# Moving the turn of the next queries and the expert-count step within a fused attention and expert-gate kernel

## The chip, the cores and the metric

The kernel runs on one core of a Trainium2 chip. The metric is the device time of one execution in microseconds (us). A profiled execution records every instruction of TensorE (matrix products), VectorE, ScalarE, GpSimd (called POOL in the profile) and SyncE (SP), and the transfers of the DMA engines. Each engine works through its own list of instructions in the order in which the program issues them, and waits at an instruction until what it needs is there.

## The reference, in short

Attention with 16 query heads over one key head and one value head, for 8 batches of 384 tokens and head dimension 64, and after it a layer of experts with two gates:

```
scores = q @ k.T / 8            # per batch b and head h: 384 x 384
attn   = softmax(scores)
x      = (attn @ v), heads side by side           # 3072 tokens x 1024
group  = argmax(x @ w_group)                      # 4 groups
expert = argmax(x @ w_expert[group])              # 4 experts in each
weight = softmax weight of group * softmax weight of expert
out    = weight * (relu(x @ w1[expert]) @ w2[expert])
```

Each token goes to one of 16 experts, each with two 1024 x 1024 matrices.

## The kernel before, in words

The attention is cut into 48 groups of 1024 score columns, two groups `g = 2p` and `g + 1` to a pair `p`, and three pairs to a batch: pair `p` is number `r = p % 3` of batch `b = p // 3`. The loop over `p` (L385) goes to 24; pass 24 only finishes pair 23. The schedule is written out by hand: instructions run on each engine in the order of the source.

What one pair does, with the helpers' names and lines:

- `load_q` (L78) brings the raw queries in on SP's queue, three pairs ahead (four transfers, three buffers); it is issued at the end of a pass, behind `stats_q` (L155, ScalarE, a sum of squares that also reads the queries). `prep_q` (L176) is VectorE's block transpose ("the turn") of the raw queries into `qT` (two buffers), which the scores of that pair need. `prep_k` (L169) does the same for the keys of a batch, `kT`, once in three pairs. `load_kv` (L85, L88) issues keys and values on ScalarE's queue at the end of each first pair of a batch.
- `scores(g, kt)` (L185, L187): score matmuls into a PSUM tile (two buffers), then ScalarE's exponential into a tile `pt` (eight buffers). There are three such calls for a group.
- `pre_add(g, 1)` (L195) and `pre_add(g, 2)` (L199): VectorE adds up the three `pt` tiles of a group into `presum`. `fold_keys(g)` (L207, L211): a block transpose `turn` and a reduction `fold`.
- `values(g)` (L232): the value matmuls of a group into `o`, two PSUM banks with one buffer. The gate's small matmuls (`gps`, `cps`, outside the unit stage `lps`) use the same buffer.
- `invert(p)` (L216 to L220): four small matmuls `sm` that need both `fold` halves of the pair, a reciprocal `rc` and its spreading `rinv`, both on VectorE. `weigh(p)` (L240, L241): VectorE multiplies `o` by `rinv` into `xT`, which frees `o`; GpSimd casts it to `xbf`.

The gate of batch `b - 1` runs in three steps during batch `b`: `gate_a` (L252, L254) in the pass with `r = 0`; `gate_b` (L261 to L293: logits, one-hot and weights) right behind it in passes below 7, and in the pass with `r = 1` otherwise; `gate_c` (L297 to L317) in the pass with `r = 1`. `gate_c` is the expert-count step: a matmul `cps` into the buffer of `o`, its reduction `cnt` on VectorE, the most frequent expert by a maximum and its index, a register load on GpSimd with the transfers of that expert's two matrices `w1` and `w2` (three transfers on GpSimd's queue, L93 and L307), and some further small VectorE instructions.

From pass 7 on (`busy`, `MOE_AT = 7`) units of the expert layer are put between: `fill(n)` issues the next `n` units, each eight matmuls (`hps` L329 or `yps` L338) and one ScalarE instruction. A batch has 14 units, and they begin with the first batch's.

The order within a pass, before the change: scores of `g`, two calls; L195; the values of the previous pair, with `sm`, `rc`, `rinv`, `xT` (in passes below 7 two score calls stand between the value groups); the third call of `g` and the first of `g + 1`; L199, `turn`, `fold` of `g`; `prep_q`; the last two score calls of `g + 1`; then the gate steps, `prep_k` and `fold_last` (L195, L199, `turn`, `fold` of `g + 1`), whose mutual order the diff shows.

Of the kernel before, what the change touches and what calls it, by code (L numbers as in the profile page):

```python
# [21 lines left out]
def kernel(  # L22
# [12 lines left out]
    B, H, S, D = q.shape  # L35
# [55 lines left out]
    def load_w1(w1, e):  # L91
        for a in range(2):
            nc.gpsimd.dma_start(out=w1[a * D:(a + 1) * D], in_=w1f[bass.ds(e, 1), a].rearrange("e p k f -> (e p) k f"))  # L93
# [73 lines left out]
    def prep_k(b):  # L167
        kT[b] = pool.tile([P, S], FP32, tag="kT", name="kT")
        nc.vector.transpose(out=kT[b][:], in_=k_raw[b][:].rearrange("p k d -> p (k d)"))  # L169

    def prep_q(p, parts=1):
        t = pool.tile([P, 2 * CW], FP32, tag="qT", bufs=2, name="qT")
        src = q_raw[p][:].rearrange("p k d -> p (k d)")
        w = 2 * CW // parts
        for i in range(parts):
            nc.vector.transpose(out=t[:, i * w:(i + 1) * w], in_=src[:, i * w:(i + 1) * w])  # L176
        qT[2 * p] = t[:, 0:CW]
        qT[2 * p + 1] = t[:, CW:2 * CW]

    def scores(g, kt):  # L180
        b = g // NCH
        ps = ps_s.tile([P, 2, CW], FP32, tag="s", name="s")
        for par in range(2):
            r = slice(64 * par, 64 * par + 64)
            nc.tensor.matmul(out=ps[:, par, :], lhsT=kT[b][r, kt * P:(kt + 1) * P], rhs=qT[g][r, :], start=True, stop=True)  # L185
        t = pool.tile([P, 2, CW], FP32, tag="pt", bufs=8, name="pt")
        nc.scalar.activation(out=t[:], in_=ps[:], func=ACTF.Exp, scale=scale)  # L187
        pt[g, kt] = t
# [3 lines left out]
    def pre_add(g, kt):  # L192
        if kt == 1:
            t = pool.tile([P, 2, CW], FP32, tag="presum", bufs=1, name="presum")
            nc.vector.tensor_add(out=t[:], in0=pt[g, 0][:], in1=pt[g, 1][:])  # L195
            presum[g] = t
        elif kt == 2:
            t = presum[g]
            nc.vector.tensor_add(out=t[:], in0=t[:], in1=pt[g, 2][:])  # L199
# [13 lines left out]
    def invert(p):  # L213
        sm = ps_m.tile([P, 32], FP32, tag="mm", name="sm")
        for par in range(2):
            nc.tensor.matmul(out=sm[64 * par:64 * par + 64, :], lhsT=sel2[:].rearrange("p a b -> p (a b)"), rhs=fold[p][:, :, 16 * par:16 * par + 16], start=True, stop=True)  # L216
        rc = pool.tile([P, 32], FP32, tag="rc", name="rc")
        nc.vector.reciprocal(out=rc[:], in_=sm[:])  # L218
        t = pool.tile([P, 2 * CW], FP32, tag="rinv", bufs=1, name="rinv")
        nc.vector.transpose(out=t[:].rearrange("p (b i) -> p b i", i=32), in_=rc[:].unsqueeze(2).to_broadcast([P, 32, 32]))  # L220
        rinv[p] = t
# [3 lines left out]
    def values(g):  # L225
        b = g // NCH
        p, ch = divmod(g, 2)
        if ch == 0:
            o_ps[p] = ps_o.tile([P, 2, CW], FP32, tag="o", name="o")
        for kt in range(ST):  # L230
            for par in range(2):
                nc.tensor.matmul(out=o_ps[p][64 * par:64 * par + 64, ch, :], lhsT=v_sb[b][:, kt, :], rhs=pt[g, kt][:, par, :], start=(kt == 0), stop=(kt == ST - 1))  # L232
# [62 lines left out]
    def gate_c(b):  # L295
        ps = ps_o.tile([P, ST, GE], FP32, tag="o", name="cps")
        nc.tensor.matmul(out=ps[:].rearrange("p s e -> p (s e)"), lhsT=ones_bf[:], rhs=ohe_t[b][:].rearrange("p s g e -> p (s g e)"), start=True, stop=True)  # L297
        cnt = pool.tile([P, GE], FP32, tag="cnt", bufs=1, name="cnt")
        nc.vector.reduce_sum(out=cnt[:], in_=ps[:].rearrange("p s e -> p e s"), axis=AX)  # L299
        top = pool.tile([P, 8], FP32, tag="top", bufs=1, name="top")  # L300
        idx = pool.tile([P, 8], U32, tag="idx", bufs=2, name="idx")
        nc.vector.max_with_indices(out_max=top[:], out_indices=idx[:], in_=cnt[:])
        reg = nc.values_load(idx[0:1, 0:1], engines=(ET.Pool,), min_val=0, max_val=GE - 1, skip_runtime_bounds_check_because="an index into 16 counts")
        w1 = wpool.tile([P, KO, F], BF16, tag="w1", name="w1")
        load_w1(w1, reg)
        w2 = wpool.tile([P, FO, Dm], BF16, tag="w2", name="w2")
        nc.gpsimd.dma_start(out=w2[:], in_=w2f[bass.ds(reg, 1)].rearrange("a p k f -> (a p) k f"))  # L307
        wts[b] = (w1, w2)
        idf = pool.tile([P, 1], FP32, tag="idf", bufs=1, name="idf")
        nc.vector.tensor_copy(out=idf[:], in_=idx[:, 0:1])  # L310
        mask = pool.tile([P, GE], FP32, tag="mask", bufs=1, name="mask")
        nc.vector.tensor_scalar(out=mask[:], in0=iota16[:], scalar1=idf[:, 0:1], scalar2=None, op0=OP.is_equal)
        nc.vector.scalar_tensor_tensor(out=extra[:, b * GE:(b + 1) * GE], in0=cnt[:], scalar=0.0, in1=mask[:], op0=OP.is_gt, op1=OP.subtract)
        gm = pool.tile([P, ST, GE], FP32, tag="gm", bufs=1, name="gm")
        nc.vector.tensor_mul(out=gm[:], in0=gate_all[:, b * GE:(b + 1) * GE, :].rearrange("p e s -> p s e"), in1=mask[:].unsqueeze(1).to_broadcast([P, ST, GE]))
        gs = pool.tile([P, ST], FP32, tag="gsel", bufs=4, name="gsel")
        nc.vector.reduce_sum(out=gs[:], in_=gm[:], axis=AX)  # L317
        gsel[b] = gs
# [40 lines left out]
    NP = NFLAT // 2  # L359
# [14 lines left out]
    def fill(n):  # L374
        while n > 0:
            if not units:
                if begun[0] >= B or begun[0] not in wts:
                    return
                units.extend(first_units(begun[0]))
                begun[0] += 1  # L380
            units.pop(0)()
            n -= 1

    MOE_AT = 7
    for p in range(NP + 1):  # L385
        b, r = divmod(p, RP)
        g = 2 * p
        busy = p >= MOE_AT
        if p < NP:
            scores(g, 0)  # L390
            scores(g, 1)
            pre_add(g, 1)
        else:
            fill(2)
        if p > 0:
            values(g - 2)
            if busy:
                values(g - 1)
                invert(p - 1)
        if p < NP:  # L400
            scores(g, 2)
            scores(g + 1, 0)
        if p > 0:
            if not busy:
                values(g - 1)
                invert(p - 1)
            weigh(p - 1)
        units_on = busy and p < NP

        if not busy:  # L410
            if p < NP:
                pre_add(g, 2)
                fold_keys(g)
            if p + 1 < NP:
                prep_q(p + 1)
        elif p < NP:
            if r == 1:
                gate_b(b - 1, between=True)
            fill(1)
            pre_add(g, 2)  # L420
            fold_keys(g)
            if p + 1 < NP:
                prep_q(p + 1)
            fill(1)
        if p < NP:
            scores(g + 1, 1)
            scores(g + 1, 2)


        def fold_last():  # L430
            if p < NP:
                pre_add(g + 1, 1)
                pre_add(g + 1, 2)
                fold_keys(g + 1)

        if not busy:
            if r == 2 and b + 1 < B:
                prep_k(b + 1)
                stats_k(b + 1)
            if r == 0 and 0 < b < B:  # L440
                gate_a(b - 1)
                gate_b(b - 1)
            if r == 1 and b > 0:
                gate_c(b - 1)
            fold_last()
        elif p < NP:
            if r == 2 and b + 1 < B:
                prep_k(b + 1)
            fold_last()
            fill(1)  # L450
            if r == 2 and b + 1 < B:
                stats_k(b + 1)
            fill(1)
            if r == 0 and 0 < b < B:
                gate_a(b - 1)
            if r == 1 and b > 0:
                gate_c(b - 1)
            fill(p % 2)
            assert not inserts
        if r == 0 and b + 1 < B:  # L460
            load_kv(b + 1)
        if p < NP:
            stats_q(p)
            if p + 3 < NP:
                load_q(p + 3)
# [254 lines left out]
```

## Time and profile before

| What | Value |
|---|---|
| Timed runs (2) | median 571.74 us, 570.04 to 573.44 |
| Profiled execution, whole time | 569.86 us |
| Its span | 567.9 us |
| TensorE matmuls busy | 496.1 us (87%) |
| VectorE busy | 369.9 us (65%) |
| ScalarE busy | 242.0 us (43%) |
| GpSimd busy | 63.8 us (11%) |
| Mean granted TensorE clock | 0.947 |

The span is the time from the first to the last recorded instruction; the whole time is a little longer. A busy share is an average over stages. Which engine sets the time of a stage is read from the waits and the timeline of that stage, not from the shares. The granted clock is given as a share of 2.4 GHz, so 0.50 is the level of 1.2 GHz.

### The profile page before, as it was taken

What the parts mean: (1) busy time and instruction counts of PE and PEld (TensorE: products, weight loads), DVE (VectorE), ACT (ScalarE), POOL (GpSimd) and SP (SyncE); (2) the same over time, 40 slices, a digit from 0 to 9 for tenths busy, and PEclk for the clock granted to TensorE, in tenths of its full rate; (3) what the DMA queues carried; (4) which work ended last, traced back from release to release, by engine and by line L of the source; (5) the groups of instructions that cost most, each with busy time, mean ns of one, the idle gap of its engine ahead of it and who ended that gap; (6) DMA issues with size and microseconds to landing.
All of it is one profiled execution on the core that took longest, in us unless ns stands there. A gap on an engine that the chain in (4) does not pass through costs nothing.

```text
span 567.9 us, 6824 instructions
## 1 busy us (share of the span) xinstructions
PE 496.1 (87%) x2521; PEld 210.1 (37%) x2521; DVE 369.9 (65%) x503; ACT 242.0 (43%) x342; POOL 63.8 (11%) x64
## 2 busy tenths in 40 slices
PE   6758677857979997999899998999899979989992
PEld 4222222313434342433443343434343434454550
DVE  2865776796979848775978496787788567241100
ACT  2434225233536444444634562556355435232331
POOL 0010011111011101110021002010111011010000
PEclk8798788879999998999999998999999989999997
DMA  9450223892359843986199529943697129689990
GB/s 122 44 67 0 38 70 47 136 213 74 59 72 216 213 96 43 199 176 160 39 165 201 171 47 143 208 154 85 99 210 176 46 45 206 176 189 236 237 253 16
DMA packets 148377, 73.06 MB, mean 129 GB/s; under 512 B 122587, under 2 KB 122587, under 8 KB 148336
## 3 DMA queue, kind: packets, MB, share of 16 engines
q0 software_dynamic: 19008, 37.84, 36.8%
q1 hardware_dynamic: 114928, 32.53, 27.1%
q10 hardware_dynamic: 14400, 2.16, 2.1%
q8 instruction: 23, 0.38, 0.3%
q14 instruction: 18, 0.15, 0.1%
HBM read 91.31 MB, written 19.40 MB: 195 GB/s over the span
## 4 chain that ended last, share of the span: by engine, by line
PE 67%; DVE 22%; issue 4%; DMA 2%; ACT 2%; SPq 1%; POOL 0%; DVEq 0%; POOLq 0%; ACTq 0%
PE o L232 23%; PE s L185 19%; PE yps L338 12%; PE hps L329 10%; DVE turn L207 4%; DVE presum L199 4%; DVE qT L176 3%; DVE presum L195 2%; DVE rinv L220 2%; DVE xT L240 2%; DMA out_dram<-y 2%; DVE fold L211 2%; PE gps L252 2%; ACT y L340 1%; DVE oh L278 1%
## 5 line engine op out<-in xcount | busy, mean ns | idle before, releaser
L187 ACT ACTIVATE pt<-s 128x1024 f32<-128x1024 f32 x144 | 140.1, 1020 | 175.0 <-PE s L185 174.9
L185 PE MATMUL s<-qT,kT 64*128 64x512 f32 x576 | 155.0, 659 | 35.6 <-DVE qT L176 17.6
L232 PE MATMUL o<-pt,v 128*64 128x512 f32 x576 | 139.8, 634 | 16.0 <-DVE cnt L299 16.0
L329 PE MATMUL hps<-xbf,w 128*128 128x384 bf16 x512 | 89.3, 326 | 2.2 <-ACT hT L331 0.9
L338 PE MATMUL yps<-w,hT 128*128 128x512 bf16 x384 | 89.5, 379 | 1.3 <-ACT y L340 1.3
L185 PEld LDWEIGHTS s<-qT,kT 64*128 64x128 f32 x576 | 53.7, 199 | 96.9 <-issue 79.6
L232 PEld LDWEIGHTS o<-pt,v 128*64 128x64 f32 x576 | 41.0, 145 | 115.3 <-issue 90.2
L195 DVE TENSOR_TENSOR presum<-pt 128x1024 f32<-128x1024 f32 x48 | 57.8, 1205 | 36.6 <-ACT pt L187 36.4
L241 POOL CAST xbf<-xT 128x1024 bf16<-128x1024 f32 x24 | 40.8, 1699 | 350.7 <-DVE xT L240 350.7
L329 PEld LDWEIGHTS <-w 128*128 128x128 bf16 x512 | 48.5, 99 | 48.1 <-issue 18.5
L207 DVE STREAM_TRANSPOSE turn<-presum 128x1024 f32<-128x1024 f32 x48 | 59.8, 1245 | 1.6
L199 DVE TENSOR_TENSOR presum<-presum,pt 128x1024 f32<-128x1024 f32 x48 | 58.6, 1221 | 2.9 <-DVE presum L195 0.5
L211 DVE TENSOR_REDUCE fold<-turn 128x32 f32<-128x1024 f32 x48 | 58.6, 1220 | 1.6
L218 DVE RECIPROCAL rc<-sm 128x32 f32<-128x32 f32 x24 | 8.6, 358 | 77.4 <-PE sm L216 77.4
L338 PEld LDWEIGHTS <-hT 128*128 128x128 bf16 x384 | 37.0, 100 | 51.9 <-issue 14.1
L340 ACT ACTIVATE y<-yps,gsel 128x512 f32<-128x512 f32 x48 | 32.9, 686 | 54.2 <-PE yps L338 49.3
L331 ACT ACTIVATE hT<-hps 128x384 bf16<-128x384 f32 x64 | 31.3, 490 | 40.2 <-PE hps L329 32.9
L176 DVE STREAM_TRANSPOSE qT<-qraw 128x1024 f32<-128x1024 f32 (+1 forms) x25 | 29.7, 1191 | 3.6 <-DMA qraw<-in_q_dram 3.6
L155 ACT ACTIVATE junk<-qraw 128x1024 bf16<-128x1024 f32 x24 | 25.2, 1052 | 14.5 <-DMA k<-in_k_dram 14.4
L220 DVE STREAM_TRANSPOSE rinv<-rc 128x1024 f32<-128x1024 f32 x24 | 29.9, 1245 | 0.8
L240 DVE TENSOR_TENSOR xT<-o,rinv 128x1024 f32<-128x1024 f32 x24 | 29.4, 1224 | 1.3
L93 POOL DMA_DIRECT2D w<-in_moe_w_dram x18 | 12.6, 706 | 101.3 <-DVE gsel L317 76.7
(123 smaller groups left out, 161.1 us busy)
## 6 DMA issues: line engine op xcount, KB each, us to landing
w<-in_moe_w_dram POOLq DMA_DIRECT2D x18, 1024.0 KB, 13.3
w<-in_moe_w_dram POOLq DMA_DIRECT2D x9, 2048.0 KB, 23.7
qraw<-in_q_dram SPq DMA_DIRECT2D x96, 128.0 KB, 3.8
out_dram<-y SPq DMA_DIRECT2D x48, 256.0 KB, 3.4
x_bf<-xbf SPq DMA_DIRECT2D x8, 768.0 KB, 3.4
k<-in_k_dram ACTq DMA_DIRECT2D x28, 48.0 KB, 2.2
v<-in_v_dram ACTq DMA_DIRECT2D x8, 96.0 KB, 2.6
xe<-x_bf SPq DMA_DIRECT2D x1, 768.0 KB, 9.5
```

Source lines behind the costliest of these rows:

```text
L176: nc.vector.transpose(out=t[:, i * w:(i + 1) * w], in_=src[:, i * w:(i + 1) * w])
L185: nc.tensor.matmul(out=ps[:, par, :], lhsT=kT[b][r, kt * P:(kt + 1) * P], rhs=qT[g][r, :], start=True, stop=True)
L187: nc.scalar.activation(out=t[:], in_=ps[:], func=ACTF.Exp, scale=scale)
L195: nc.vector.tensor_add(out=t[:], in0=pt[g, 0][:], in1=pt[g, 1][:])
L199: nc.vector.tensor_add(out=t[:], in0=t[:], in1=pt[g, 2][:])
L207: nc.vector.transpose(out=t[:], in_=presum[g][:].rearrange("p a n -> p (a n)"))
L211: nc.vector.reduce_sum(out=fold[p][:, ch, :], in_=t[:].rearrange("p (b i) -> p b i", i=32), axis=AX)
L220: nc.vector.transpose(out=t[:].rearrange("p (b i) -> p b i", i=32), in_=rc[:].unsqueeze(2).to_broadcast([P, 32, 32]))
L232: nc.tensor.matmul(out=o_ps[p][64 * par:64 * par + 64, ch, :], lhsT=v_sb[b][:, kt, :], rhs=pt[g, kt][:, par, :], start=(kt == 0), stop=(kt ...
L241: nc.gpsimd.tensor_copy(out=xbf[b][:, cs], in_=xT[b][:, cs])
L329: nc.tensor.matmul(out=ps[:, 0:S], lhsT=w1[:, ko, fc * P:(fc + 1) * P], rhs=xb[:, ko * S:(ko + 1) * S], start=(ko == 0), stop=(ko == KO - 1))
L338: nc.tensor.matmul(out=ps[:], lhsT=state["h"][:, fo, st * P:(st + 1) * P], rhs=w2[:, fo, nh * CW:(nh + 1) * CW], start=(fo == 0), stop=(fo ...
```

## The change

`prep_q(p + 1)` and, in the last pair of a batch, `prep_k(b + 1)` are issued right behind the first key addition of the pass (L195 of `g`), in all passes with a next pair. Before, `prep_q` stood behind `fold` of `g` and `prep_k` ahead of `fold_last`. `stats_k` stays where it was. In passes from 7 on with `r = 1`, `gate_c` is issued ahead of `fold_last` and ahead of the units that follow; before, it stood behind `fold_last` and two units. Nothing that is computed changes.

```diff
             scores(g, 0)
             scores(g, 1)
             pre_add(g, 1)
+            if p + 1 < NP:
+                prep_q(p + 1)
+            if r == 2 and b + 1 < B:
+                prep_k(b + 1)
         else:
             fill(2)
...
             if p < NP:
                 pre_add(g, 2)
                 fold_keys(g)
-            if p + 1 < NP:
-                prep_q(p + 1)
         elif p < NP:
             if r == 1:
                 gate_b(b - 1, between=True)
             fill(1)
             pre_add(g, 2)
             fold_keys(g)
-            if p + 1 < NP:
-                prep_q(p + 1)
             fill(1)
...
         if not busy:
             if r == 2 and b + 1 < B:
-                prep_k(b + 1)
                 stats_k(b + 1)
...
         elif p < NP:
-            if r == 2 and b + 1 < B:
-                prep_k(b + 1)
+            if r == 1 and b > 0:
+                gate_c(b - 1)
             fold_last()
             fill(1)
             if r == 2 and b + 1 < B:
                 stats_k(b + 1)
             fill(1)
             if r == 0 and 0 < b < B:
                 gate_a(b - 1)
-            if r == 1 and b > 0:
-                gate_c(b - 1)
             fill(p % 2)
```

## Rows read from the trace of the kernel before

**Rows 1.** Waits of TensorE: us in total, times, longest us.

```profile
PE s L185 <- DVE qT L176: 17.6, 7, 6.0
PE o L232 <- DVE cnt L299: 16.0, 6, 3.0
PE s L185 <- DVE kT L169: 12.9, 2, 6.5
PE s L185 <- DVE cnt L299: 4.7, 1, 4.7
```

**Rows 2.** Timeline, one early pair: start us, us, engine, line; idle before in brackets.

```profile
107.96 1.99 PE L185 MATMUL s<-qT,kT 64*128 64x512 f32 x8
109.88 2.79 PE L232 MATMUL o<-pt,v 128*64 128x512 f32 x12
...
112.81 0.36 DVE L218 RECIPROCAL rc<-sm 128x32 f32<-128x32 f32 x1 [3.28 <-PE sm L216]
...
114.48 1.22 DVE L240 TENSOR_TENSOR xT<-o,rinv 128x1024 f32<-128x1024 f32 x1
...
119.29 1.23 DVE L176 STREAM_TRANSPOSE qT<-qraw 128x1024 f32<-128x1024 f32 x1
120.45 0.53 DVE L169 STREAM_TRANSPOSE kT<-k 128x384 f32<-128x384 f32 x1
...
121.13 3.79 PE L185 MATMUL s<-qT,kT 64*128 64x512 f32 x8 [6.45 <-DVE kT L169]
```

**Rows 3.** Windows: stretch, busy us by engine, granted clock, DMA share, GB/s.

```profile
119.00:123.00 4.00, 1.87 (x5) 0.94 (x7) 3.90 (x5) 0.00 (x0) 0.00 (x0) 0.50 1.17 214
...
127.00:131.00 4.00, 4.00 (x18) 1.17 (x16) 0.24 (x1) 1.94 (x2) 0.00 (x0) 1.00 0.71 106
```

**Rows 4.** Chain of waits, value matmuls in passes 8 and 11: start us, us.

```profile
163.86 5.37 PE o L232 x24
...
223.36 7.07 PE o L232 x24
```

**Rows 5.** Timeline of VectorE: count step and last key additions of pair 4.

```profile
101.71 0.17 DVE L299 TENSOR_REDUCE cnt<-cps 128x16 f32<-128x48 f32 x1
...
103.32 1.22 DVE L195 TENSOR_TENSOR presum<-pt 128x1024 f32<-128x1024 f32 x1
...
108.32 1.22 DVE L195 TENSOR_TENSOR presum<-pt 128x1024 f32<-128x1024 f32 x1
```

**Rows 6.** Timeline: first L195 of pair 1, and `sm` of pair 6.

```profile
25.45 1.23 DVE L195 TENSOR_TENSOR presum<-pt 128x1024 f32<-128x1024 f32 x1
...
147.49 0.26 PE L216 MATMUL sm<-fold,sel 128*64 128x32 f32 x4
```

**Rows 7.** Timeline of pair 6: gate computation's start, what follows it, next exponentials.

```profile
140.24 0.18 DVE L273 COPY L<-lps 128x60 f32<-128x60 f32 x1
...
142.24 1.22 DVE L195 TENSOR_TENSOR presum<-pt 128x1024 f32<-128x1024 f32 x1
...
144.68 1.92 ACT L187 ACTIVATE pt<-s 128x1024 f32<-128x1024 f32 x2
```

**Rows 8.** Timeline of TensorE, scores ahead of pass 11.

```profile
218.37 1.99 PE L185 MATMUL s<-qT,kT 64*128 64x512 f32 x8 [0.86 <-DVE qT L176]
```

**Rows 9.** Timeline of TensorE, first scores of passes 4 and 7.

```profile
81.50 3.78 PE L185 MATMUL s<-qT,kT 64*128 64x512 f32 x8 [1.83 <-DVE qT L176]
...
140.37 1.99 PE L185 MATMUL s<-qT,kT 64*128 64x512 f32 x8 [1.79 <-DVE qT L176]
```

**Rows 10.** DMA issues: line, count, KB each, median us to landing.

```profile
w<-in_moe_w_dram POOLq DMA_DIRECT2D x9, 2048.0 KB, 23.7
```

**Rows 11.** Timeline, query loads on SP's queue and pair 5's sum of squares ending.

```profile
99.69 28.72 SPq L78 DMA_DIRECT2D qraw<-in_q_dram  x5
...
117.31 0.19 ACT L155 ACTIVATION_READ_ACCUMULATOR junk<-qraw 128x1 f32 x1
```

**Rows 12.** The raw queries' tile: its transfers.

```profile
DMA to landing us min/median/max: 2.4/3.8/11.9
```

## The prediction

> **What bounds the kernel now.** I read the waits of TensorE first, because TensorE is the busiest engine of the page. Nearly all its long waits in the attention loop end on VectorE: 17.6 us on `qT` (L176), 12.9 on `kT` (L169), 16.0 and 4.7 on `cnt` (L299) [rows 1]. So the question is what stands in front of these three in VectorE's program order, and the timeline of VectorE answers it.
>
> The loop has two stages. In pairs 0 to 6 no expert units run. There the timeline of one pair [rows 2] reads as one chain: `rc` at 112.81, five more VectorE steps (`rinv`, `xT`, second key addition, `turn`, `fold`), `qT` at 119.29, `kT`, and only then TensorE's next scores at 121.13, after 6.45 us without a matmul. Those eight score matmuls take 3.79 us where eight earlier ones took 1.99: the granted clock is 0.50 (the 1.2 GHz level) in the stretch that follows the idle one, and 1.00 (2.4 GHz) four microseconds on [rows 2, 3]. The scores need nothing of `rc` to `fold`; they stand behind them only through `qT`.
>
> In pairs 7 to 23 expert units fill TensorE. The chain of waits [rows 4] passes there through the 24 value matmuls `o` of the pair after each count step. They wait for `cnt` because counts and values share one PSUM buffer, and `cnt` stands behind the five steps of the last key additions. Six such waits make the 16.0 us [rows 1]. Three of the six `o` groups then take 7.07 us instead of 5.37.
>
> **The change, part by part, pairs 0 to 6.** `prep_q` moves ahead of `rc`. Its load was issued two pairs earlier and its destination was last read by scores that precede those feeding L195, so I cost the turn at its own 1.23 us and no wait (bounded under the rivals). What is late next? With `qT` early, TensorE may run the next pair's first two scores right behind this pair's last two. VectorE then has no idle time left, because what it waited for, `sm`, comes while it is adding and turning. One round of VectorE, step by step:
> - L195 1.22 [rows 5] and `qT` 1.23 [rows 2];
> - `rc` to the end of `fold`: 119.29 - 112.81 = 6.48 [rows 2];
> - the second group's L195, L199, `turn`, `fold`: 108.32 - 103.32 = 5.00 [rows 5];
> - sum 13.93 us.
>
> TensorE needs less: three times 1.99 for scores and twice 2.79 for values, 11.6 us [rows 2]. Placing it against `rc` at T: its scores end by about T+2, values wait for `xT` at T+2.9 (114.48 + 1.22 - 112.81) [rows 2], and 2.79 + 1.99 + 2.79 later, at T+10.5, it waits for the last `fold` at T+11.5. Two gaps of about 1 us each, off VectorE's path. ScalarE's six exponentials and one sum of squares fit between.
>
> From the first L195 of pair 1, at 25.45, to `sm` of pair 6, at 147.49, the old kernel takes 122.0 us [rows 6]. The new one: 6 x 13.93 = 83.6; two `kT` at 0.53 make 1.1 [rows 2]; two gate computations of 142.24 - 140.24 = 2.0 make 4.0 [rows 7]; one count step 103.32 - 101.71 = 1.6 [rows 5]. In pair 3 the exponentials for pair 4 stay behind the gate's own: they end 6.4 us after `L` starts (144.68 + 1.92 - 140.24) [rows 7], the first near T+11.9; a score, six values and `sm` follow, T+16.8, where VectorE would be ready at T+15.9: 0.9 more. In pair 6 both value groups precede those scores, so nothing. Sum 91.2: a gain of **30.8 us**. Pair 0 does the same VectorE work in another order and gains nothing before 25.45.
>
> **Pairs 7 to 23.** `qT` in front of `rc` costs 1.23 us on VectorE, `kT` 0.53 in one pair of three. The cover is the 5.37 us of value matmuls during which `rc` waits for `sm` [rows 4]. Without it `xT` comes 1.8 us later, and next wanted is its PSUM buffer, by the count matmul or the next values, more than 10 us on. So nothing. `prep_k` moved needs keys loaded two pairs ahead: nothing.
>
> `gate_c` moves ahead of the last additions on VectorE, and on TensorE ahead of two or three units. The new wait is `cps` for the gate's one-hot; behind it on TensorE stand those units. The gate computation follows `xT` directly and TensorE has two units and two scores in between, so I cost it at nothing; unhidden it would be a few tenths, six times. Its Pool part moves along: one register load and three weight transfers, issued about 5 us earlier, behind which the next `xbf` cast stands with over 10 us to spare. SP's queue is passed by nothing. On VectorE the 1.6 us [rows 5] now delay `fold`, hence `sm`. But `cnt` comes 5 us earlier and the values behind it take 5.37 us, in which L195 to `fold` (5.00) fits, just.
>
> Gone are therefore the six waits, 16.0 us [rows 1]; the low clock behind three of them, 3 x (7.07 - 5.37) = 5.1 [rows 4]; and one wait of scores for `qT`, 0.9 [rows 8]. That makes **22.0 us**.
>
> **The sum.** 30.8 + 22.0 = 52.8. The profiled execution took 569.86 us (its span of 567.9 and 1.96 around it); 569.9 - 52.8 = 517.1. The median of the two timed runs stands 1.9 above that execution.
>
> **The clock, weighed.** The low level costs an early pair 1.8 us on eight scores [rows 2]; with the values after it at most about 3. It follows long idle stretches as a rule, but the rows hold two pairs with the gate's matmuls, where three shorter gaps, the last of 1.83 and 1.79 us, precede the scores: once these take 3.78 us, once 1.99 for eight [rows 9]. My early pairs leave two gaps of about 1 us, and one of about 3 ahead of the gate's matmuls in pairs 3 and 6. I take full clock except half a us each in those two pairs, rounding 517.1 up to 518, and keep 6 x 3 = 18 us as the other end. The Trainium skill, page "TensorE: Matmul & The Clock Gate", section "A second HAM failure mode: psum-queue depth-cycling", speaks against me: it reports that short idles between groups of matmuls, repeated often enough, also make the clock swing. By that rule the sum would come out near 530 instead of 517; the low start at 81.50 agrees with it, the full one at 140.37 does not, so the trace leaves it open.
>
> **Rivals.**
> 1. The clock drops in every early pair. TensorE's round becomes 11.6 + 3 = 14.6, above VectorE's 13.93, and the delays add to the handovers: 3 to 18 us more, 520 to 535. For it: most old early pairs start low. Against: those follow gaps of up to 6 us [rows 1], mine are of about 1.
> 2. The first expert's weights are late. Pair 7's first unit needs them. They are issued right after pair 4's `cnt`, which in my schedule is 25.45 + three rounds + 8.93 of the fourth (up to its `fold`) + 0.5 for `kT` + 2.9 for the gate of pair 3 = 79.6 us, and land 23.7 us later at the median [rows 10], near 105; the unit starts near 118. Only if the transfer took over 38 us would the early gain be given back. Price: up to some 10 us, 527.
> 3. The reciprocal's delay reaches TensorE after all: 23 turns at 1.23 and seven `kT` at 0.53, together 32 us, on the path: 549. For it: `xT` holds the buffer that values need. Against: after `sm` TensorE has four scores to run, about 4 us, more than `xT`'s 2.9 and nearly all of it.
> 4. Slower: the turn waits for its queries and VectorE, in order, holds `rc`, `xT` and both additions behind it. For it: query loads issued beside the weights drag on; the five from 99.69 take 28.72 us to issue, the longest landing is 11.9 [rows 11, 12]. From the end of the square sum that lets the last four go (117.31 + 0.19) to the latest landing, 99.69 + 28.72 + 11.9 = 140.3, are 22.8 us. In my schedule `rc` of pair 5 starts at 89.2 by the same sum and the squares end some 3.4 later, 92.6; the turn wants the queries at 25.45 + 91.2 + 1.2 = 117.8: 25 us, 2 us to spare. This decides from there: if each of the 23 turns waited 3 us, 69 us would come on top, 586. Against: most loads land in 3.8 us [rows 12], and the weights are under way in less than half of each three pairs.
> 5. Another engine's order keeps the old pace: the scores are really held by something else that ends when `qT` does. Then about 22 us or less remain, 548 to 565. Against: 121.13 follows `kT` immediately, and the waits name it.
>
> **Chances and range.** Forecast 0.70 (own range 511 to 524: half a us per early pair either way, the gate pairs, and the cover of `cnt`), rival 1 0.14, rival 2 0.03, rival 3 0.05, rival 4 0.03, rival 5 0.05. Two per cent, 11 us, is about what a measurement can tell from no change. Faster by more: the forecast, rivals 1 to 3 and over half of rival 5, 0.94; within: 0.03; slower: 0.03. For 8 in 10 I take the forecast's low end and rival 1 to its upper end: 509 to 534.
>
> **What would show it.** In the changed profile: `qT` right behind L195, and `rc` with almost no idle time before it in pairs 1 to 6; `sm` of pair 6 near 117; rounds of 14 us; a full clock there; no value matmul waiting for `cnt`; every `o` group of 24 at 5.37. I am wrong if the early rounds stay near 20 us, if `qT` waits for a transfer, or if the values now wait for `xT` in the unit pairs.

## The result and the profile after

The changed kernel takes 525.03 us (median of two runs, 524.29 and 525.78) against 571.74; the ratio is 0.918, interval 0.909 to 0.927. In a later group of four runs it took 523.42 us against 574.33: 0.910, interval 0.908 to 0.913. The forecast of 518 is 7 us too low, inside its range of 509 to 534. The profiled execution took 524.29 us, 7.2 more than the 517.1 of the sum.

The waits answer [rows 1] first (engine and line that waited, for whom: us in total, times, longest):

```profile
DVE qT L176 <- DMA qraw<-in_q_dram: 31.5, 6, 7.0
...
DVE rc L218 <- PE sm L216: 10.4, 4, 7.1
...
PE yps L338 <- DVE rc L218: 5.1, 4, 2.1
PE s L185 <- DVE qT L176: 3.6, 1, 3.6
...
PE o L232 <- DVE cnt L299: 1.7, 1, 1.7
...
PE hps L329 <- DVE L L273: 1.1, 2, 0.9
...
PE s L185 <- DVE kT L169: 0.6, 1, 0.6
```

Of the waits of [rows 1] little is left: 3.6 us on `qT`, which are the first load of all, 0.6 on `kT`, and 1.7 for `cnt`, in pair 4. Two things are new: VectorE waits 31.5 us for raw queries, where it waited 3.6 before, and TensorE's units wait 5.1 us for `rc`.

Now the early pairs, beside [rows 2, 5, 6], from the timeline (start us, us, engine, line; idle before in brackets):

```profile
25.24 1.22 DVE L195 TENSOR_TENSOR presum<-pt 128x1024 f32<-128x1024 f32 x1
...
86.30 1.22 DVE L195 TENSOR_TENSOR presum<-pt 128x1024 f32<-128x1024 f32 x1
...
87.43 1.24 DVE L176 STREAM_TRANSPOSE qT<-qraw 128x1024 f32<-128x1024 f32 x1
...
88.59 0.54 DVE L169 STREAM_TRANSPOSE kT<-k 128x384 f32<-128x384 f32 x1
89.05 0.32 DVE L218 RECIPROCAL rc<-sm 128x32 f32<-128x32 f32 x1
...
89.62 2.04 PE L185 MATMUL s<-qT,kT 64*128 64x512 f32 x8 [0.27 <-ACT pt L187]
...
100.48 1.22 DVE L195 TENSOR_TENSOR presum<-pt 128x1024 f32<-128x1024 f32 x1
...
117.16 0.31 PE L216 MATMUL sm<-fold,sel 128*64 128x32 f32 x4
```

A round of VectorE, from one first addition to the next, is 100.48 - 86.30 = 14.18 us, `kT` in it; no instruction of it waits. The next pair's scores start 0.57 us after `rc` does, after 0.27 us of idle time and at 2.04 us for eight. `sm` of pair 6 stands at 117.16, where 116.7 was worked out. The clock of the busy stretches is full (windows: stretch, busy us by engine, granted clock, DMA share, GB/s):

```profile
88.00:98.00 10.00, 9.44 (x44) 2.90 (x42) 9.76 (x10) 7.35 (x10) 1.97 (x1) 1.00 1.15 212
160.00:180.00 20.00, 20.00 (x109) 7.95 (x108) 14.35 (x13) 10.08 (x13) 1.97 (x1) 1.00 0.54 148
```

The new waits are in the unit stage. Passes 13 to 15 of the changed kernel, from the timeline:

```profile
243.37 1.37 POOL L93 DMA_DIRECT2D w<-in_moe_w_dram  x2 [6.84 <-DVE gsel L317]
...
244.87 20.51 SPq L78 DMA_DIRECT2D qraw<-in_q_dram  x4
...
266.88 0.26 PE L216 MATMUL sm<-fold,sel 128*64 128x32 f32 x4
...
271.44 1.25 DVE L176 STREAM_TRANSPOSE qT<-qraw 128x1024 f32<-128x1024 f32 x1 [6.95 <-DMA qraw<-in_q_dram]
272.61 0.32 DVE L218 RECIPROCAL rc<-sm 128x32 f32<-128x32 f32 x1
272.98 1.89 PE L338 MATMUL yps<-w,hT 128*128 128x512 bf16 x8 [2.09 <-DVE rc L218]
```

And the kernel before, at the same two steps of pass 13 (the loads, and the weights behind them):

```profile
281.50 2.27 SPq L78 DMA_DIRECT2D qraw<-in_q_dram  x4
...
285.57 1.37 POOL L93 DMA_DIRECT2D w<-in_moe_w_dram  x2 [12.96 <-DVE gsel L317]
```

Before, the four query transfers of this pass were issued within 2.27 us and the weights 4 us later. Now the weights come 1.5 us ahead, and the four take 20.51 us to issue. The longest landing of a query transfer rose from 11.9 [rows 12] to 25.1 us:

```profile
DMA to landing us min/median/max: 2.4/3.8/25.1
```

The Trainium skill, page "Trainium Kernel Development and Optimization", section "Key Constraints", says that transfers issued from SP, ScalarE and GpSimd run on the same 16 DMA engines and interleave; 20.51 us against 2.27 agrees. Two passes later the turn wants these queries and waits 6.95 us. `sm` has been ready since 267 and `rc`, behind the turn, comes at 272.61. `sm` lies in one of the two PSUM buffers that the units use as well, so the unit's matmuls wait for `rc`.

### The profile page after: what moved, and what is told of

The parts are those of the page before. It is cut to its first block, busy times and chain, and to the rows that moved or that the text cites. A ratio compares the mean times of both kernels' runs of the same rounds, so it can differ in the third digit from the quotient of the medians.

```text
span 522.3 us, 6814 instructions
## 1 busy us (share of the span) xinstructions
PE 480.7 (92%) x2521; PEld 203.6 (39%) x2521; DVE 369.3 (71%) x503; ACT 240.5 (46%) x342; POOL 63.8 (12%) x64
## 4 chain that ended last, share of the span: by engine, by line
PE 49%; DMA 18%; DVE 15%; SPq 7%; ACT 4%; issue 4%; ACTq 1%; POOL 0%; DVEq 0%; POOLq 0%
DMA qraw<-in_q_dram 15%; PE yps L338 13%; PE s L185 12%; PE hps L329 12%; PE o L232 9%; SPq L78 6%; PE gps L252 3%; DVE qT L176 2%; DVE presum L195 2%; DVE turn L207 2%; DMA out_dram<-y 2%; DVE presum L199 2%; DVE rinv L220 2%; DVE xT L240 2%; ACT junk L155 1%
## 5 line engine op out<-in xcount | busy, mean ns | idle before, releaser
L185 PE MATMUL s<-qT,kT 64*128 64x512 f32 x576 | 145.1, 623 | 6.2 <-DVE qT L176 3.6
L232 PE MATMUL o<-pt,v 128*64 128x512 f32 x576 | 130.2, 597 | 2.7 <-DVE cnt L299 1.7
L195 DVE TENSOR_TENSOR presum<-pt 128x1024 f32<-128x1024 f32 x48 | 58.5, 1219 | 29.7 <-ACT pt L187 29.6
L185 PEld LDWEIGHTS s<-qT,kT 64*128 64x128 f32 x576 | 49.7, 187 | 65.6 <-issue 41.8
L232 PEld LDWEIGHTS o<-pt,v 128*64 128x64 f32 x576 | 38.7, 136 | 90.4 <-issue 73.9
L176 DVE STREAM_TRANSPOSE qT<-qraw 128x1024 f32<-128x1024 f32 (+1 forms) x25 | 29.8, 1196 | 31.5 <-DMA qraw<-in_q_dram 31.5
L155 ACT ACTIVATE junk<-qraw 128x1024 bf16<-128x1024 f32 x24 | 25.2, 1052 | 14.7 <-DMA k<-in_k_dram 12.5
L252 PE MATMUL gps<-xT,gw 128*32 128x384 f32 x128 | 14.5, 580 | 5.8 <-DVE xT L240 2.9
```

## The experiments

Theory A was: VectorE sets the early pace; TensorE alone paid for `cnt`; and the missing 6 to 7 us come from weights that now precede query loads, through the turn, `rc` and the PSUM buffer of `sm`. The runs were made in three groups, each with the kernel before beside it; there it took 574.25, 570.08 and 574.33 us in the median.

**The parts alone.** The count step alone, in the unit passes of the kernel before; both turns stay where they were:

```
+            if r == 1 and b > 0:
+                gate_c(b - 1)
             fold_last()
...
-            if r == 1 and b > 0:
-                gate_c(b - 1)
```

> Only the count step is moved; the turns stay at their old place. Theory A (the six waits for cnt and the low clock behind three of them were TensorE's alone): the early pairs stay as before, sm of pair 6 near 147.5; no value matmul waits for cnt; gain 16.0 + 5.1 = 21 us, 549 against 570 profiled. VectorE's waits for queries stay under 4 us, because the turn comes some 10 us later in the pair. Rival B (weight transfers issued ahead of the query loads cost time by themselves, wherever the turn stands): VectorE waits for queries over 10 us and the gain is under 16 us.

Measured: 550.85 us (548.66 to 553.64), ratio 0.962, interval 0.952 to 0.972. Its waits:

```profile
PE s L185 <- DVE cnt L299: 6.0, 3, 4.7
...
DVE qT L176 <- DMA qraw<-in_q_dram: 3.4, 1, 3.4
```

No value matmul waits for `cnt` (4.7 of the 6.0 us are those of pair 4 in [rows 1]), and VectorE waits for the first queries only. The loads are as late here as with the whole change, the longest landing is 25.7 us, but the turn comes after them. So the weights ahead of the loads cost no wait while the turn stands late: B falls. The profiled run took 552.65 us, 17.2 less than before, where 21 were forecast. `sm` of pair 6 stands at 151.55, 4.1 us later than in [rows 6], though nothing ahead of it was changed. Of these, 3.0 us are pass 7 at the low clock: its first scores took 3.78 us, which in the run of [rows 9] took 1.99, and the 24 value matmuls behind them 6.60 instead of 5.37.

The turns alone, the changed kernel with the count step back behind the additions in the unit passes:

```
-            if r == 1 and b > 0:
-                gate_c(b - 1)
             fold_last()
...
+            if r == 1 and b > 0:
+                gate_c(b - 1)
```

> Only the turns of queries and keys are moved; the count step stays behind the last additions. Theory A: sm of pair 6 near 117, as with the whole change; the waits for cnt remain, six of about 3 us; with the weight transfers again issued behind the query loads VectorE's waits for queries fall from 31.5 us to under 8; gain 30 to 33 us, 537 to 540 profiled. Rival C (the turn, gone from between the additions, already brings cnt forward far enough): waits for cnt under 8 us, 528 to 532.

Measured: 534.72 us (532.61 to 536.22), ratio 0.934, interval 0.924 to 0.943.

```profile
PE o L232 <- DVE cnt L299: 14.7, 7, 3.2
...
DVE qT L176 <- DMA qraw<-in_q_dram: 3.5, 1, 3.5
```

The waits for `cnt` remain, 14.7 us with the 1.7 of pair 4, so 13.0 in the unit passes against 16.0. The turn no longer stands ahead of the count, which shortens some of them, and the time is a little below A's 537 to 540: A holds, and C for a fifth. `sm` of pair 6 stands at 120.04 where 117 was forecast. Again VectorE does not wait for later queries. The long query waits need both parts: weights ahead of the loads and an early turn.

**What the late queries cost.** Three kernels keep the whole change and break the path, two at the late loads and one at `rc`. First, a fourth buffer and the loads ahead of the count step (the loads at the end of the pass are then left out; not shown):

```
-        t = pool.tile([P, NBP, 32], FP32, tag="qraw", bufs=3, ...)
+        t = pool.tile([P, NBP, 32], FP32, tag="qraw", bufs=4, ...)
...
             if r == 1 and b > 0:
+                if p + 3 < NP:
+                    load_q(p + 3)
                 gate_c(b - 1)
```

> The whole change, with a fourth buffer of raw queries and, in the unit passes with r = 1, the query loads issued ahead of the count step. Theory A (the weights, now issued ahead of the query loads, make these late; VectorE waits at the turn with rc behind it, and rc holds the PSUM buffer of sm that the units need): VectorE's waits for queries fall from 31.5 to about 4 us (the first one stays), TensorE's waits for rc from 5.1 to under 1; 519 to 521 profiled against 524.3. Rival D (the turn's own 1.2 us ahead of rc makes rc late): TensorE's waits for rc stay near 5, no change.

Measured: 517.47 us (517.03 to 518.37), ratio 0.904, interval 0.896 to 0.913. VectorE's only wait for queries is the first:

```profile
DVE qT L176 <- DMA qraw<-in_q_dram: 3.8, 1, 3.8
```

TensorE's wait for `rc` is gone, with the turn still ahead of `rc`: D falls. The longest landing is still 24.6 us. Now it is the next pass's loads that come behind the weights (those of pass 14 take 20.34 us to issue), and the turn wants them a pass later. On a second chip, beside the changed kernel:

> The whole change again, as the yardstick on one chip for the two kernels beside it. All theories: 524 to 526; VectorE waits about 31 us for queries, TensorE about 5 us for rc.

> The kernel with a fourth raw query buffer and the loads ahead of the count step, again, beside the whole change. Theory A: 517 to 518, 1.2 to 1.6% below the whole change.

Measured: 523.42 us (522.14 to 524.24) for the change, ratio 0.910, interval 0.908 to 0.913; 519.12 us (517.78 to 520.11) with the loads first, ratio 0.903, interval 0.901 to 0.905. In the change VectorE waits 31.8 us for queries and TensorE 5.2 us for `rc`, as the first time. The difference is 4.3 us, 0.8%, less than the 7.6 between the first medians and less than A's 1.2 to 1.6%, but the intervals don't meet. The clock hides part of it: with the loads first, this profiled execution lost 4.1 us in the early pairs against the earlier one (last section).

Second, the weights held back until the next queries are there, with three buffers (`late` holds the register load and the three weight transfers):

```
...
+                nc.gpsimd.tensor_copy(out=gate[:], in_=q_raw[p + 3][:, 0, 0:1])
+            late.pop(0)()
```

> The whole change with three query buffers as before; in the unit passes only the weight transfers of the count step are held: GpSimd issues them at the end of the pass, behind a small copy that waits until the next query load has landed. Theory A (it is the order of the two transfers, not the number of buffers, that matters): VectorE's waits for queries fall from 31 to about 4 us, TensorE's waits for rc to under 1; 517 to 520. Rival J (the fourth buffer, by which loads no longer wait for the sum of squares, is what helped): waits stay above 15 us, 523 to 526.

Measured: 520.09 us (519.71 to 521.37), ratio 0.905, interval 0.903 to 0.907, on that second chip: at the upper end of A's 517 to 520, and clear of the change. From its waits and its groups of instructions (count, busy us, mean ns, idle before):

```profile
DVE qT L176 <- DMA qraw<-in_q_dram: 3.8, 1, 3.8
```

```profile
L475 POOL COPY wgate<-qraw 128x1 f32<-128x1 f32 x5 | 1.7, 343 | 66.3 <-DMA qraw<-in_q_dram 66.3
```

GpSimd now does the waiting, neither TensorE nor VectorE nor ScalarE waits for the weights, and TensorE's waits for `rc` are gone. The gain over the change is 3.3 us. So it is the order of the two transfers that matters; J falls.

Third, the turn behind `rc`, with the loads still late (`mid` is `prep_q(p + 1)` in the passes with units):

```
         nc.vector.reciprocal(out=rc[:], in_=sm[:])
+        if mid is not None:
+            mid()
```

> The whole change, but in the passes with units the turn stands between rc and rinv. Theory A (it is rc, held behind the turn, that keeps the PSUM buffer of sm from the units): the turn still waits for its queries, about 14 us in these passes and 3.4 at the start, but TensorE's waits for rc fall from 5.1 to under 0.5 us; 518 to 521. Rival F (TensorE loses the 5 us through xT or the additions that the late turn holds as well): waits of about 5 us under another name, 523 to 526.

Measured: 520.31 us (517.88 to 521.52), ratio 0.910, interval 0.902 to 0.917. The same place as above, in this kernel's timeline, and its waits:

```profile
266.48 0.26 PE L216 MATMUL sm<-fold,sel 128*64 128x32 f32 x4
266.79 0.36 DVE L218 RECIPROCAL rc<-sm 128x32 f32<-128x32 f32 x1 [2.70 <-PE sm L216]
...
270.22 1.25 DVE L176 STREAM_TRANSPOSE qT<-qraw 128x1024 f32<-128x1024 f32 x1 [3.07 <-DMA qraw<-in_q_dram]
```

```profile
DVE qT L176 <- DMA qraw<-in_q_dram: 16.3, 6, 3.8
```

The turn still waits, 16.3 us in all where 17 were forecast, and everything but `rc` stands behind it; yet TensorE has no wait for `rc`. `sm` of pair 6 stands at 117.16 as in the change, so the 5.1 us between the two profiled executions (519.18 and 524.29) lie behind it. This is the link that was in doubt: it is `rc`, hence the buffer of `sm`, and not `xT` or the additions. F falls for these 5 us.

The turn at its old place in the unit passes tells less, since it removes the wait for queries and the turn ahead of `rc` at once:

```
-            if p + 1 < NP:
+            if p + 1 < NP and not busy:
                 prep_q(p + 1)
```

> The whole change, but in the passes with units (7 and later) the turn of the queries stands at its old place behind fold of g. Theory A: the early gain stays (sm of pair 6 near 117); rc no longer stands behind the turn, TensorE's waits for rc go from 5.1 to under 0.5; the turn itself may still wait for queries, up to 10 us in all, off the path; 518 to 521 profiled. Rival E (scores of the next pair wait for the turn again, as before the change): TensorE's waits for qT over 3 us, 522 to 526.

Measured: 518.92 us (517.74 to 520.66), ratio 0.907. VectorE's waits for later queries and TensorE's for `rc` are both gone; E falls.

**Who sets the early pace.** One more transpose of VectorE at the end of pairs 1 to 6, in the changed kernel and in the one before:

```
             fold_last()
+            if p > 0:
+                x = pool.tile([P, 2 * CW], FP32, tag="turn", bufs=1, name="turn")
+                nc.vector.transpose(out=x[:], in_=presum[g + 1][:] ...)
```

> The whole change with one more block transpose of 128 x 1024 (about 1.25 us, its result is not used) on VectorE at the end of each of the pairs 1 to 6. Theory A (with the change VectorE sets the pace of the early pairs): sm of pair 6 comes 6 x 1.25 = 7.5 us later than 117.2, less about 1 hidden in pair 3 where VectorE waits 1.1 us for sm; 531 to 533. Rival G (TensorE or ScalarE sets the pace there): under 2 us later.

> The kernel before with the same extra transpose at the same place. Theory A: before the change VectorE waits 3 to 5 us for sm in each of these pairs, so the transpose is hidden in pairs 1 to 5; only behind pair 6, where rc waits for nothing, it may cost its 1.25 us: 0 to 1.5 us. Rival G: as with the change, 6 us or more.

Measured: 532.55 us (531.34 to 533.48) with the change, 7.5 above 525.03; 574.12 us without it, ratio to the kernel before 1.0046, interval 1.0006 to 1.0086, so 0.3 to 4.9 us. In the first nothing hides them; here is the first of the six in VectorE's timeline, the next pair's addition behind it, and `sm` of pair 6:

```profile
40.00 1.25 DVE L447 STREAM_TRANSPOSE turn<-presum 128x1024 f32<-128x1024 f32 x1
41.35 1.23 DVE L195 TENSOR_TENSOR presum<-pt 128x1024 f32<-128x1024 f32 x1
...
126.69 0.25 PE L216 MATMUL sm<-fold,sel 128*64 128x32 f32 x4
```

That is 9.5 us later than 117.16, where 6.5 were forecast. The excess is of the size of the clock's part: TensorE now idles 4.4 us instead of 2.9 ahead of the gate's matmuls in pairs 3 and 6, and the eight scores behind them take 3.60 and 3.79 us, where they take 1.99 in the changed kernel.

In the second VectorE's wait for `sm` shrinks from 77.4 us to 73.4 and the profiled run has pass 7 at the low clock:

```profile
140.69 3.78 PE L185 MATMUL s<-qT,kT 64*128 64x512 f32 x8 [1.78 <-DVE qT L176]
...
150.83 0.25 PE L216 MATMUL sm<-fold,sel 128*64 128x32 f32 x4
```

This run's low start alone accounts for 3.78 - 1.99 = 1.8 us beside [rows 9]. The count-only run has the same low start and, up to there, the same instructions without the extra transposes, and its `sm` of pair 6 comes no earlier:

```profile
151.55 0.26 PE L216 MATMUL sm<-fold,sel 128*64 128x32 f32 x4
```

So VectorE sets the pace with the change, G falls for it, and before the change most of the extra work at least was hidden. The 2.6 us by which the timed runs are longer are no more than the clock alone does at this place; how much of them is transpose stays open.

Taking work from VectorE instead, on top of the loads-first kernel:

```
+        eng = nc.gpsimd if g % 2 and 2 < g < 2 * MOE_AT else nc.vector
...
-            t = pool.tile([P, 2, CW], FP32, tag="presum", bufs=1, name="presum")
-            nc.vector.tensor_add(...)
+            t = pool.tile([P, 2, CW], FP32, tag="presum", bufs=2, name="presum")
+            eng.tensor_add(...)
```

> The kernel with four raw query buffers and loads ahead of the count step (517.5), with the first and second key additions' partial work split: in pairs 1 to 6 the first addition of the second group runs on GpSimd into a second presum buffer. Theory A (VectorE sets the early pace): 1.2 us less per pair, 6 to 7 us, 510 to 512, if GpSimd's addition is ready in time. Rival H (the two engines slow each other, or the addition on GpSimd is late): 514 or more.

Measured: 522.14 us (520.33 to 522.75), ratio 0.912: slower than 517.47, a miss for A's number. Timeline of pair 4, waits:

```profile
82.97 2.41 POOL L197 TENSOR_TENSOR presum<-pt 128x1024 f32<-128x1024 f32 x1
85.41 1.23 DVE L201 TENSOR_TENSOR presum<-presum,pt 128x1024 f32<-128x1024 f32 x1 [5.26 <-POOL presum L197]
```

```profile
DVE presum L201 <- POOL presum L197: 7.4, 4, 5.3
```

GpSimd's addition stands behind its cast and, in pair 4, behind the issue of the weight transfers; VectorE waits 7.4 us for it, which gives back the six additions saved (7.3 us). H holds in its second form, lateness. What VectorE runs beside GpSimd's addition, `turn` and `fold`, keeps its 1.25 and 1.22 us; none of its own additions runs beside it, so whether two additions slow each other is not shown. Of the 4.7 us beyond, part is clock (0.74 granted from 100 to 120 us of its span); the rest is not settled.

**The two stages apart.** In every profiled execution the span can be cut at `sm` of pair 6, where the early pairs end.

| Kernel | `sm` of pair 6 at, us | from there to the end of the span, us |
|---|---|---|
| before | 147.49 | 420.4 |
| count step alone | 151.55 | 398.5 |
| turns alone | 120.04 | 413.8 |
| whole change | 117.16 | 405.1 |
| whole change, again | 116.38 | 405.1 |
| loads first | 116.69 | 398.8 |
| loads first, again | 120.78 | 397.4 |
| weights held | 120.19 | 399.5 |
| turn behind `rc` | 117.16 | 400.1 |
| turn late in the unit passes | 119.05 | 398.7 |

Behind `sm` the prediction comes to 420.4 - 22.0 = 398.4 us. The count step alone reaches that; the whole change misses it by 6.7 us, and each kernel that breaks the path comes back to within 1.7. The turns alone gain 6.6 us there, because they shorten the same waits for `cnt`: the gains of the two parts do not add up.

## Why the prediction was right, and where 7 us went

- **Early pairs, 30.8 us:** `sm` of pair 6 moved from 147.49 to 117.16, 30.3 us. The sum over VectorE's steps was right to half a us, and the two runs with the extra transpose show that this engine is the bound. That it came so close is partly luck with the clock: in the eight profiled executions with these early pairs `sm` stands at 116.38 to 120.78.
- **The gate pair, 0.9 us:** forecast as a wait for the exponentials; TensorE waits 0.9 us for one in pair 3, and VectorE 1.1 us for `sm`.
- **The count step, 16.0 + 5.1 us, and 0.9:** the waits of value matmuls in the unit passes are gone, and with them the 7.07 us groups; behind `sm` of pair 6 the count step alone gains 21.9 us, where 22.0 were forecast. One reading was loose: `cnt` stood behind four steps of the last key additions and the turn of the queries, so that the turn's move alone took the waits from 16.0 to 13.0 us.
- **What failed** is the end of the same part: "SP's queue is passed by nothing", and the weight transfers "issued about 5 us earlier" costed at no more than a waiting cast. They were moved past the query loads of their own pass, on the DMA engines if not in a queue, and `qT` then waited for a transfer, which the prediction had named as a sign of being wrong. The second half is "next wanted is its PSUM buffer, by the count matmul or the next values": that looked at the buffer of `o` alone and left out that `rc` frees the buffer of `sm`. Together they cost 5.1 us of waits for `rc`, of the 6.7 us missing behind `sm` of pair 6; early pairs give the other 0.5. With the loads first 6.3 of the 6.7 come back, with only `rc` moved 5.0, so about 1 us of what the late queries cost is not traced. The units' new waits for the gate's logits `L`, 1.1 us, are another matter: 0.9 of them stand in pass 7, ahead of any late query in the unit passes, and are there in the first run with the loads first too.
- **Rival 4** had the mechanism (the turn waits, all of VectorE behind it) but was tried only where the first weights load, before pair 7's turn; there it held, with no wait. Its size was bounded by landings of 11.9 us, taken while weights came behind the loads. Of 31.5 us that VectorE waited, 5.1 reached TensorE as waits for `rc`.
- **The clock:** rival 1 did not come. The short gaps of the early pairs, 0.3 to 1.7 us, left the clock at 1.00. The Trainium skill's report on repeated short idles ("TensorE: Matmul & The Clock Gate", "A second HAM failure mode: psum-queue depth-cycling") is not borne out by this pattern. The clock fell in the idle stretches of 2.9 us ahead of the gate's matmuls in pairs 3 and 6 (0.50 from 58 to 61 us and from 106 to 108). These matmuls took 2.75 and 2.79 us, against 1.66 at full clock in another execution: about 1.1 us each, where half a us was taken.
- **The range:** 525.03 us lies just above the forecast's own range of 511 to 524. It is inside 509 to 534 because that range was widened for the clock, which is not what was missing.

The lowest medians are those of the whole change with the query loads ahead of the count step: 517.47 and 519.12 us on the two chips. The late turn in the unit passes (518.92) and the held weights (520.09) overlap with it in their runs.

## What to carry to other kernels

When a step is moved, list its transfers and ask which transfers of other queues they now precede: these share the DMA engines, and a prefetch that was early enough behind nothing may be late behind 4 MB of weights. When an instruction that can wait for data is put ahead of another, ask for every buffer which the second frees, small shared PSUM tiles too. And a chain of one engine's steps, added up from the trace, forecasts the pace well once no other wait is left in it.

## What the runs showed of the hardware that was not expected

The same kernel, with the loads first, ran the eight scores behind the gate's matmuls (L252) of pair 6 at full clock in one profiled execution and at the low one in another. One, then the other, from `sm` of pair 5 to `sm` of pair 6:

```profile
100.16 0.31 PE L216 MATMUL sm<-fold,sel 128*64 128x32 f32 x4 [1.22 <-DVE fold L211]
...
105.31 2.79 PE L252 MATMUL gps<-xT,gw 128*32 128x384 f32 x16 [2.93 <-DVE xT L240]
...
109.48 1.99 PE L185 MATMUL s<-qT,kT 64*128 64x512 f32 x8
...
116.69 0.31 PE L216 MATMUL sm<-fold,sel 128*64 128x32 f32 x4
```

```profile
102.74 0.31 PE L216 MATMUL sm<-fold,sel 128*64 128x32 f32 x4 [1.22 <-DVE fold L211]
...
107.90 1.66 PE L252 MATMUL gps<-xT,gw 128*32 128x384 f32 x16 [2.93 <-DVE xT L240]
...
111.56 3.79 PE L185 MATMUL s<-qT,kT 64*128 64x512 f32 x8
...
120.78 0.25 PE L216 MATMUL sm<-fold,sel 128*64 128x32 f32 x4
```

Ahead of both TensorE stood idle for 2.9 us before the gate's first matmul and 0.6 before its second group. The clock fell in both, but not at the same point: in the first the gate's matmuls ran at the low level and the scores at full clock again, in the second the gate's matmuls at full clock and the scores at the low level. From one `sm` to the next the second takes 18.04 us against 16.53, so 1.5 us more. The other 2.6 of the 4.1 us between the two `sm` of pair 6 were lost before, the same way: from 60 to 70 us, around the gate of pair 3, the granted clock was 0.59 against 1.00. So executions of one kernel differ by some us from these two places alone.
